# One transformer block on one core: big tiles at multiples of 512 bytes, one throw-away area for the score maxima

## The chip, the core and the metric

The kernel runs on one core of a Trainium2 chip. The core has four compute engines that run side by side, each with its own queue of instructions: TensorE (PE in the profile, with its weight loads as PEld), VectorE (DVE), ScalarE (ACT) and GpSimd (POOL). SyncE (SP) issues the DMA transfers here. Engines wait for each other by semaphores. SBUF, the working memory, has 128 partitions; a tile in it is an area of so many bytes in every partition, and "where a tile begins" is its offset in bytes within the partition. PSUM holds eight banks, in which PE accumulates its products (bank 0 to bank 7).

The metric is device time in microseconds (us) of one execution. Before the change it is 705.58 us, the median of 3 runs (704.65 to 707.68).

## The reference: what is computed

One pre-norm transformer block for 2048 tokens of width 448, in float32:

```
h   = x + attention(layernorm(x)) @ wo      # 16 heads of 28, causal window of 256 tokens
out = h + (gelu(n @ w_gate) * (n @ w_up)) @ w_down,  n = layernorm(h)     # inner width 1792
scores = (q @ k.T) / sqrt(28), outside the window -1e9, then softmax, then @ v
```

## The kernel before

**Arithmetic.** PE reads numbers that ACT has rounded ("high half", `to_hi` at L390) and, as a second operand, what is left over of the float32 number (the "low half", `to_lo` at L393, mostly on DVE). A product is then a sum of three: high by high, high by low and low by high.

**Stages.** The tokens lie in 16 tiles of 128. (1) Layer norm and the projection to q, k and v (L672, L618), with weights and tokens split in halves. (2) Attention, in 16 blocks B, each of 4 heads and 512 tokens. (3) The output projection (L894) and the sum into `hres`, the residual, which stays in SBUF as 16 x 448 floats per partition. (4) The second layer norm. (5) The feed-forward part in pairs of weight slices: products with the gate and up weights (L1128 and L1140 for the first pairs, L1329 for the others), GELU and the product on ACT, DVE and POOL, and the product with the down weights (L1403), whose results DVE adds into `hres` (L1420). The stages overlap: projections still run beside the first blocks of attention, the first feed-forward products beside the last ones. In the trace the scores of stage (2) run from about 40 to about 300 us, and the feed-forward part has PE for itself from about 312 us on.

**A block of attention.** For each of its 4 token tiles i and 4 heads j, PE computes 128 rows of scores against up to three key tiles (L723) into a PSUM bank. DVE adds the mask and takes the maximum of each row with one `tensor_tensor_reduce` (L727). Two things come out of that instruction: the maxima, into a column of `mx`, and the masked scores themselves, which nobody reads. These are written to `junk`. There are 16 of these steps per block, 256 in all, of 384 columns or fewer; in the built program each stands as two rows, the custom instruction and the reading of its accumulator. From `mx` DVE makes the high and low half of the maxima (L744, L747), PE turns them (L754), ACT puts them as further rows into `rq` (L390), and a second product (L798) then gives scores less their maximum, with keys down the partitions. ACT takes the exponent (L802), POOL sets what is outside the window to zero (L817), PE multiplies by v (L836).

**Where the buffers lie.** Three pools of tiles share SBUF. The main pool holds `hres`, `xT` (normed tokens, turned), `proj` (projection weights, later feed-forward weights and activations), `raw`, `v`, `xn` and small ones, and starts at the left. The pool "late" follows it: `rk1`, `rq1` (keys and queries of odd blocks), `mt` (the mask in columns 0 to 383, and the throw-away areas behind it), `pp` (probabilities), `oblk`, `oT`, `wos`, `ohl`; for the feed-forward part its place is taken by `xo` (tokens, turned) and `gh` (activations). The pool "even" grows from the right-hand end: `rk0` and `rq0` (even blocks), and later in their place `w2` and `e0` to `e3`. Feed-forward weights lie by turns in `w2` and in two areas of `proj`; in the profile's rows `w2` is called `w`, and the high halves of activations lie in `e` or `gh` or in parts of `xT`. PSUM banks 0 and 1 take the scores, and bank 7 as well once the projections are done.

**What sets the order.** The kernel computes the order itself. Each piece of work is put on a list with an engine, an assumed cost, a key (how early it is wanted) and the names it reads and writes; a list scheduler (class `Lists`) then writes the instructions out, engine by engine, and the framework keeps that order and adds the semaphores. Those it works out from the memory that the instructions touch. The scheduler's own names are apart from this: the score maxima are listed with a name `("junk", s % 2)` that they only read, before and after the change.

The lines that the change touches beside those in the functions below:

```
 276  last_hi = pool.tile([128, 128], F32R, name="lasthi")      # high half of a part of the turned tokens
 305  rp.tile([128, 88], F32, name="pad0")                      # ahead of rk0, rq0
 319  p.tile([128, 88], F32, name="pad1")                       # ahead of w2, e0 .. e3
 336  junk = [mt[:, 384 + 192 * i:576 + 192 * i].bitcast(BF) for i in range(2)]
```

Of the kernel before, what the change touches and what calls it, by code (L numbers as in the profile page):

```python
# [8 lines left out]
F32 = mybir.dt.float32  # L9
F32R = mybir.dt.float32r  # L10
BF = mybir.dt.bfloat16
# [79 lines left out]
def mm(n):  # L91
    return max(n / 2400 + 0.0155, 0.115)
# [14 lines left out]
class Lists:  # L107
# [6 lines left out]
    def op(self, eng, cost, lat, key, fn, r=(), w=(), bank=None, port=False, size=0, tag=None, after=(), part=None, mode=0):  # L114
        o = Op()
        o.eng, o.cost, o.lat, o.key, o.fn, o.port, o.size, o.tag, o.mode = eng, cost, lat, key, fn, port, size, tag, mode
        o.deps, o.users, o.ready, o.start = set(after), [], 0.0, None
        o.banks = () if bank is None else tuple(bank) if type(bank) is list else (bank,)
        for b in o.banks:
            b.left += 1  # L120
        held = o.banks if part is None else [(b, *part) for b in o.banks]
        if eng == "pe":
            w = (*w, *held)
        else:
            r = (*r, *held)
        for toks, wr in ((r, False), (w, True)):
            for tok in toks:
                spans = type(tok) is tuple and (tok[0] in SPANS or type(tok[0]) is Bank)
                name, lo, hi = tok if spans else (tok, 0, 1)
                old = self.seen.setdefault(name, [])  # L130
                keep = []
                for a in old:
                    if a[0] < hi and lo < a[1] and a[2] is not o:
                        if wr or a[3]:
                            o.deps.add(a[2])
                        if wr and lo <= a[0] and a[1] <= hi:
                            continue
                    keep.append(a)
                keep.append((lo, hi, o, wr))
                self.seen[name] = keep  # L140
        for d in o.deps:
            d.users.append(o)
        self.ops.append(o)
        if tag is not None:
            self.open[tag] = self.open.get(tag, 0) + 1
            self.all.setdefault(tag, []).append(o)
        return o
# [104 lines left out]
def block_kernel(ctx: ExitStack, tc, x, wqk_in, wv_in, wo_in, gu_in, rest_in, cw_in, down_in, out):  # L252
    nc = tc.nc
# [5 lines left out]
    pool = ctx.enter_context(tc.tile_pool(name="main", bufs=1))  # L259
# [4 lines left out]
        return ap.bitcast(F32)  # L264


    hres = pool.tile([128, NT, D], F32, name="hres")
    xT = pool.tile([128, 7, S], F32R, name="xT")
    proj_m = pool.tile([128, 7936], F32R, name="proj")
# [3 lines left out]
    xn = [xn_m[:, D * i:D * i + D] for i in range(2)]  # L273
    ident = pool.tile([128, 128], F32, name="ident")
    one_r = pool.tile([128, 128], F32R, name="one")
    last_hi = pool.tile([128, 128], F32R, name="lasthi")


    kept_m = pool.tile([128, 96], F32, name="kept")
# [19 lines left out]
    bank = [psum.tile([128, 512], F32, name=f"bank{i}") for i in range(8)]  # L299
# [2 lines left out]
    fst, snd = ExitStack(), ExitStack()  # L302
    lp = fst.enter_context(tc.tile_pool(name="late", bufs=1))
    rp = snd.enter_context(tc.tile_pool(name="even", bufs=1, side="right"))
    rp.tile([128, 88], F32, name="pad0")
    rks = [p.tile([128, 3072], F32R, name=f"rk{u}") for u, p in enumerate((rp, lp))]
    rqs = [p.tile([128, 2048], F32R, name=f"rq{u}") for u, p in enumerate((rp, lp))]
    mt = lp.tile([128, 768], F32, name="mt")
    pp_m = lp.tile([128, 4 * PPB * 128], F32, name="pp")
    oblk = lp.tile([128, 512], F32, name="oblk")  # L310
# [5 lines left out]
    def open_even():  # L316
        snd.close()
        p = ctx.enter_context(tc.tile_pool(name="ev", bufs=1, side="right"))
        p.tile([128, 88], F32, name="pad1")
        ev.append(p.tile([128, 3072], F32R, name="w2"))  # L320
        ev.extend(p.tile([128, 512], F32R if i > 1 else F32, name=f"e{i}") for i in range(4))

    def open_late():
        fst.close()
        p = ctx.enter_context(tc.tile_pool(name="fp", bufs=1))
        late.append(p.tile([128, 26 * 512], F32R, name="xo"))
        late.append(p.tile([128, 2, 2, 512], F32R, name="gh"))
# [5 lines left out]

    v = v_m[:, 0:8 * VT].rearrange("p (t h d) -> p t h d", t=8, h=H)
    mask = mt[:, 0:384]
    junk = [mt[:, 384 + 192 * i:576 + 192 * i].bitcast(BF) for i in range(2)]
    kept = [m.rearrange("p (b r) -> p b r", r=12) for m in (v_m[:, 8 * VT:8 * VT + 96], kept_m)]


# [350 lines left out]
    def block(B):  # L690
        return B % 4, B // 4
# [23 lines left out]
    def scores(B, i, j):  # L715
        g, c = block(B)
        u, m0 = B % 2, i if c else max(i, 2)
        b = Bank("score")
        o = (m0 - i) * 128
        s = 16 * B + 4 * i + j  # L720

        def one():
            nc.tensor.matmul(bank[b.k][:, o:384], rq[u][0:3 * DH, j, i * 128:i * 128 + 128],  # L723
                             rk[u][0:3 * DH, j, m0 * 128:(i + 3) * 128], start=True, stop=True)

        def most():
            nc.vector.tensor_tensor_reduce(junk[s % 2][:, o:384], bank[b.k][:, o:384], mask[:, o:384],  # L727
                                           1.0, -BIG, OP.add, OP.max, mx[:, i, j:j + 1])
        op("pe", mm(384 - o), 0.19 + (384 - o) / 2400, s, one,
           [("rq", u, i), *(("rk", u, m) for m in range(m0, i + 3))],  # L730
           (), b, tag="score")
        op("dve", 0.08 + (384 - o) * 0.00104, 0.165 + (384 - o) * 0.00106, s, most, ["mask", ("junk", s % 2)],
           [("mx", i, j)], b, tag="most")
# [883 lines left out]
    for c in range(CS):  # L1617
# [17 lines left out]
        for g in range(NG):  # L1635
# [30 lines left out]
            if B == 14:  # L1666
                op("py", 0, 0, 0, open_even, (), ["evenring"], after=[o for tag in ("score", "prob", "most", "tr", "rx") for o in L.all[tag]])
# [112 lines left out]
```

## Time and profile before

| what | value |
|---|---|
| median of 3 runs | 705.58 us (704.65 to 707.68) |
| the profiled execution | 707.69 us, of which the span from first to last instruction is 706.0 us |
| PE busy | 693.6 us, 98% of the span |
| DVE busy | 501.8 us, 71% |
| ACT / POOL busy | 414.7 us, 59% / 325.5 us, 46% |
| mean granted TensorE clock | 0.998 of full speed |
| stages: busy time of PE / DVE | 0 to 40 us: 37.2 / 31.7; 40 to 312 us: 272.0 / 211.6; 312 to 384 us: 69.4 / 44.2; 384 to 706 us: 315.0 / 214.2 |

How to read the rows that follow. A row of an instruction gives its start and its duration in us, its engine, the line of the kernel, the operation, and what it writes from what it reads. A row of a group gives a line, an engine, an operation and the tiles, the number of instructions (x), then busy time in us and the mean duration of one in ns, then the idle time of the engine just before them. A row of a stretch of time gives the stretch, the busy time of each engine with the number of instructions, the granted clock, the share of the DMA engines in use and what they moved. A row of waits says which engine waited at which tile and line, for whom, and how long: in all, how often, and the longest. "The chain" is the work that ended last, followed back from the last instruction to whatever released each step.

### The profile page before, as it was taken

To read this page: it belongs to the slowest core of one execution; us is meant where nothing else is said; L and a number is where in the kernel's file an instruction comes from. 1 tells how busy PE (TensorE), PEld (TensorE's weight loads), DVE (VectorE), ACT (ScalarE), POOL (GpSimd) and SP (SyncE) were. 2 spreads that over 40 slices of the span, in tenths; PEclk is the share of its full clock that TensorE was granted. 3 is DMA by queue.
4 is the path that set the end of the run, shared out by engine and by line. 5 is a ranking of instruction groups with operands and counts; after the bars stand their busy time and mean duration, and the time that the engine had idled before them with its cause. 6 is when DMAs were issued, how large, how long until landed. Compare 5 with 4: busy or idle time off the path is not lost.

```text
span 706.0 us, 15432 instructions
## 1 busy us (share of the span) xinstructions
PE 693.6 (98%) x5544; PEld 583.7 (83%) x5544; DVE 501.8 (71%) x1194; ACT 414.7 (59%) x911; POOL 325.5 (46%) x441
## 2 busy tenths in 40 slices
PE   8999999999999999999989999999999999999997
PEld 7887888877888787778778887888898888888886
DVE  7966668987796689838637677875745755865764
ACT  7746676877677666875544656635535445546431
POOL 5613544554546346441554678624403546657000
PEclk9999999999999999999999999999999999999999
DMA  8896967987678776306775866504304653442102
GB/s 310 269 292 187 294 176 216 217 233 189 193 228 222 211 206 173 109 1 163 197 194 174 243 187 188 148 15 129 89 1 128 188 165 121 139 145 86 42 15 104
DMA packets 104691, 116.25 MB, mean 165 GB/s; under 512 B 44632, under 2 KB 82392, under 8 KB 104040
## 3 DMA queue, kind: packets, MB, share of 16 engines
q1 hardware_dynamic: 104472, 115.17, 56.7%
q8 instruction: 43, 0.70, 0.4%
q14 instruction: 32, 0.26, 0.1%
q10 hardware_dynamic: 144, 0.11, 0.0%
HBM read 84.97 MB, written 44.47 MB: 183 GB/s over the span
## 4 chain that ended last, share of the span: by engine, by line
PE 92%; DVE 3%; DMA 2%; ACT 1%; issue 1%; SPq 0%; POOL 0%; DVEq 0%; ACTq 0%
PE bank L1329 26%; PE bank L1403 17%; PE bank L672 9%; PE bank L798 7%; PE bank L723 7%; PE bank L1128 6%; PE bank L836 6%; PE bank L894 5%; PE bank L618 5%; PE bank L1140 2%; DMA pp<-in_wv_dram 1%; DVE hres L1420 1%; DMA xn<-v 1%; PE bank L448 0%; DMA hres<-in_x_dram 0%
## 5 line engine op out<-in xcount | busy, mean ns | idle before, releaser
L727 DVE CUSTOM_DVE_ANT_0 mt<-bank,mt 128x384 bf16<-128x384 f32 (+2 forms) x256 | 127.0, 526 | 26.2 <-PE bank L723 24.1
L802 ACT ACTIVATE pp<-bank 128x384 f32<-128x384 f32 (+1 forms) x212 | 105.0, 536 | 26.6 <-PE bank L798 23.0
L817 POOL TENSOR_SCALAR_AFFINE_SELECT pp<-pp 128x512 f32<-128x512 f32 x120 | 75.9, 647 | 87.4 <-ACT pp L802 81.9
L1329 PE MATMUL bank<-xT,proj 64*128 64x512 f32 x735 | 94.5, 389 | 0.0
L672 PE MATMUL bank<-xT 128*128 128x512 f32 x308 | 93.0, 399 | 0.0
L1329 PEld LDWEIGHTS bank<-xT,proj 64*128 64x128 f32 x735 | 72.9, 184 | 11.9 <-ACT e L1249 0.4
L723 PE MATMUL bank<-rk,rq 84*128 84x384 f32 (+2 forms) x256 | 81.1, 340 | 0.0
L798 PE MATMUL bank<-rq,rk 104*128 104x384 f32 (+2 forms) x352 | 80.7, 305 | 0.0
L1403 PE MATMUL bank<-proj,gh 64*128 64x448 f32 x624 | 72.2, 363 | 0.1
L798 PEld LDWEIGHTS bank<-rq,rk 104*128 104x128 f32 x352 | 58.8, 189 | 12.2 <-ACT pp L802 3.6
L1420 DVE TENSOR_TENSOR hres<-bank,hres 128x448 f32<-128x448 f32 (+1 forms) x113 | 62.8, 611 | 5.8 <-PE bank L1403 5.7
L1403 PEld LDWEIGHTS bank<-proj,gh 64*128 64x128 f32 x624 | 60.0, 184 | 6.9 <-ACT e L1249 1.2
L1249 ACT ACTIVATE e<-bank 1x1 f32<-1x1 f32 x139 | 21.8, 157 | 69.6 <-PE bank L1403 45.7
L672 PEld LDWEIGHTS bank<-xT 128*128 128x128 f32 x308 | 55.7, 189 | 7.5 <-DVE proj L393 0.5
L723 PEld LDWEIGHTS bank<-rk,rq 84*128 84x128 f32 x256 | 47.0, 189 | 11.7 <-DVE xn L484 1.9
L1199 POOL TENSOR_TENSOR xn<-proj 128x384 f32<-128x384 f32 (+2 forms) x36 | 34.5, 961 | 46.5 <-DVE e L393 19.0
L390 ACT ACTIVATE rq<-bank 8x512 fp32r<-8x512 f32 x64 | 37.6, 588 | 23.2 <-PE bank L754 22.2
L618 PE MATMUL bank<-proj,xT 128*128 128x448 f32 (+1 forms) x220 | 50.0, 333 | 0.0
L1329 PE MATMUL bank<-xo,proj 64*128 64x512 f32 x366 | 48.1, 389 | 0.2 <-ACT e L1249 0.2
L393 DVE TENSOR_TENSOR proj<-proj 128x448 fp32r<-128x448 f32 (+2 forms) x32 | 24.0, 761 | 31.1 <-ACT proj L390 28.8
L836 PE MATMUL bank<-pp,v 128*29 128x384 f32 (+2 forms) x704 | 44.6, 387 | 0.0
L1403 PE MATMUL bank<-proj,xT 64*128 64x448 f32 x312 | 38.4, 368 | 4.4 <-ACT e L1249 2.5
(176 smaller groups left out, 1414.9 us busy)
## 6 DMA issues: line engine op xcount, KB each, us to landing
rk<-k SPq DMA_DIRECT2D x44, 336.0 KB
rq<-q SPq DMA_DIRECT2D x32, 336.0 KB
gu<-in_gu_dram SPq DMA_DIRECT2D x18, 480.0 KB
proj<-gu SPq DMA_DIRECT2D x24, 288.0 KB
q<-proj SPq DMA_DIRECT2D x12, 448.0 KB
proj<-down SPq DMA_DIRECT2D x22, 224.0 KB
proj<-gu SPq DMA_DIRECT2D x24, 192.0 KB
k<-proj SPq DMA_DIRECT2D x9, 448.0 KB
```

The lines of the kernel that those rows point to most:

```text
L618: op("pe", mm(224 * n), 0.29 if n == 1 else 0.38, key + a / 16, lambda a=a, h=h, wb=wb, xb=xb: nc.tensor.matmul(bank[b.k][:, 0:224 * n], x ...
L672: op("pe", mm(512) + 0.002, 0.403, key, lambda a=a, h=h, wb=wb, xb=xb: nc.tensor.matmul(bank[b.k], wqk[m][:, h, wb, :], xT[:, xb, cc * 128 ...
L723: nc.tensor.matmul(bank[b.k][:, o:384], rq[u][0:3 * DH, j, i * 128:i * 128 + 128], rk[u][0:3 * DH, j, m0 * 128:(i + 3) * 128], start=True, ...
L727: nc.vector.tensor_tensor_reduce(junk[s % 2][:, o:384], bank[b.k][:, o:384], mask[:, o:384], 1.0, -BIG, OP.add, OP.max, mx[:, i, j:j + 1])
L798: nc.tensor.matmul(bank[b.k][:, n * i:n * i + n], rk[u][0:104, j + i, m * 128:m * 128 + 128], rq[u][0:104, j + i, lo * 128:(hi + 1) * 128] ...
L802: nc.scalar.activation(pp[:, j:j + G, o * 128:o * 128 + n], bank[b.k][:, 0:G * n].rearrange("p (g t) -> p g t", g=G), AF.Exp, scale=SCALE)
L817: nc.gpsimd.affine_select(a, a, pattern=[[0, 4], [-cm, 128]], compare_op=op_, fill=0.0, base=0, channel_multiplier=cm)
L836: nc.tensor.matmul(bank[b.k][32 * j:32 * j + DH + 1, lo * 128:(hi + 1) * 128], v[:, at_v(4 * c - 2 + m), 4 * g + j, :], pp[:, j, at[m] * 1 ...
L1128: nc.tensor.matmul(bank[banks[side ^ ph].k], cwbuf[n % 4][0]()[HALF[side], o:o + 128], carea(c, xl, j, side), start=not ph and not j and n ...
L1329: nc.tensor.matmul(bank[b.k], w, xarea(u.cp, xl, xs, side)[:, xk], start=p in (1, 2, 5) and not k and not t, stop=t == 2, tile_position=(6 ...
L1403: nc.tensor.matmul(bank[banks[q].k][:, 0:D], h[oh][0]()[HALF[x], q * 128:q * 128 + 128], d[wh][0]()[HALF[x]], start=not ph and not y and n ...
L1420: op("dve", 0.07 + w * 0.463 / D, 0.163 + w * 0.463 / D, key, lambda: nc.vector.tensor_tensor(hres[:, t, c0:c0 + w], bank[b.k][:, c0:c0 + ...
```

## The change

```diff
--- before.py
+++ after.py
@@ -264,6 +264,7 @@
+    pool.tile([128, 96], F32, name="pad2")
     hres = pool.tile([128, NT, D], F32, name="hres")
     xT = pool.tile([128, 7, S], F32R, name="xT")
     proj_m = pool.tile([128, 7936], F32R, name="proj")
@@ -273,7 +274,6 @@
     ident = pool.tile([128, 128], F32, name="ident")
     one_r = pool.tile([128, 128], F32R, name="one")
-    last_hi = pool.tile([128, 128], F32R, name="lasthi")
@@ -302,9 +302,9 @@
     rp = snd.enter_context(tc.tile_pool(name="even", bufs=1, side="right"))
-    rp.tile([128, 88], F32, name="pad0")
     rks = [p.tile([128, 3072], F32R, name=f"rk{u}") for u, p in enumerate((rp, lp))]
     rqs = [p.tile([128, 2048], F32R, name=f"rq{u}") for u, p in enumerate((rp, lp))]
+    rp.tile([128, 120], F32, name="pad0")
@@ -316,9 +316,9 @@
-        p.tile([128, 88], F32, name="pad1")
         ev.append(p.tile([128, 3072], F32R, name="w2"))
         ev.extend(p.tile([128, 512], F32R if i > 1 else F32, name=f"e{i}") for i in range(4))
+        p.tile([128, 120], F32, name="pad1")
@@ -333,7 +333,8 @@
     mask = mt[:, 0:384]
-    junk = [mt[:, 384 + 192 * i:576 + 192 * i].bitcast(BF) for i in range(2)]
+    junk = mt[:, 384:576].bitcast(BF)
+    last_hi = mt[:, 576:704].bitcast(F32R)
@@ -724,7 +725,7 @@
-            nc.vector.tensor_tensor_reduce(junk[s % 2][:, o:384], bank[b.k][:, o:384], mask[:, o:384],
+            nc.vector.tensor_tensor_reduce(junk[:, o:384], bank[b.k][:, o:384], mask[:, o:384],
                                            1.0, -BIG, OP.add, OP.max, mx[:, i, j:j + 1])
```

**Where the tiles begin**, in bytes within the partition, as the remainder by 512, read from the built programs:

| tiles | before | after |
|---|---|---|
| `hres`, `xT`, `proj`, `raw`, `rk1`/`xo`, `rq1`, `mt`, `pp`, `oblk`, `oT`, `wos`, `ohl`/`gh` | 128 | 0 |
| `rk0`/`w2`, `rq0`/`e0` to `e3` | 480 | 0 |
| `v` | 384 | 256 |
| `xn`, `ident`, `one` | 256 | 128 |
| the halves of the maxima, `mhl` | 384 | 256 |

The new 384 bytes ahead of `hres` move the left-hand side. On the right-hand side a pool's tiles are packed against the end of SBUF in the order of their making, the last one outermost, so that a pad makes a difference to `rk0`, `rq0`, `w2` and `e` only if it is made after them. The 512 bytes of `last_hi` come out of the main pool; the tile now uses the part of `mt` that was the second throw-away area.

**One throw-away area.** Before, maximum s wrote its masked scores to area s % 2; now all of them write to the same 384 bf16 columns. Two maxima that follow each other now write the same memory, so the framework orders them by a semaphore, although both are on DVE and stand in the same order as before. On DVE's queue, early in attention (two low halves of tokens, then maxima from bank 0 and bank 1; `mt` is the tile with mask and throw-away area), there stands before:

```order
L393 TENSOR_TENSOR xT<-bank_178,xT 128x3x128 [waits Activation_49]
L393 TENSOR_TENSOR xT<-bank_178,xT 64x128
L727 ISA mt,mx<-bank_172,mt 128x384 [waits PE_49]
L727 ISA mx 128x1
L727 ISA mt,mx<-bank_173,mt 128x384 [waits PE_49]
```

and after (lines are one higher there):

```order
L394 TENSOR_TENSOR xT<-bank_178,xT 128x3x128 [waits Activation_49]
L394 TENSOR_TENSOR xT<-bank_178,xT 64x128
L728 ISA mt,mx<-bank_172,mt 128x384 [waits DVE_49,PE_49]
L728 ISA mx 128x1
L728 ISA mt,mx<-bank_173,mt 128x384 [waits DVE_49,PE_49]
```

No instruction has moved; each maximum waits for DVE itself beside PE. An instruction of this program carries one semaphore to wait for, and a second one becomes a semaphore instruction ahead of it: DVE has 1,648 instructions in the built program instead of 1,454. The order of PE, POOL, ACT and SP is the same as before, and so are the waits of PE, POOL and SP.

## The prediction

> **What bounds the kernel now.** I read the head of the page first, then the chain that ended last, then the busy time by stretches, then the instructions one by one.
>
> ```profile
> span 706.0 us, 15432 instructions
> PE 693.6 (98%) x5544; PEld 583.7 (83%) x5544; DVE 501.8 (71%) x1194; ACT 414.7 (59%) x911; POOL 325.5 (46%) x441
> PE 92%; DVE 3%; DMA 2%; ACT 1%; issue 1%; SPq 0%; POOL 0%; DVEq 0%; ACTq 0%
> ```
>
> PE is busy in 98% of the span and carries 92% of the chain. So a nanosecond of PE's pace counts, and so does any moment in which PE waits for another engine; work elsewhere counts only through such a wait. The change touches both: it moves the tiles that PE reads, and it ties each score maximum on VectorE (DVE) to the one before it. The attention phase, where the maxima are, has these rows (columns: PE, PEld, DVE, ACT, POOL busy, clock, DMA share, GB/s):
>
> ```profile
> 40.00:300.00 260.00, 259.97 (x1805) 209.41 (x1804) 207.02 (x701) 182.74 (x360) 123.77 (x204) 1.00 0.75 209
> 120.00:130.00 10.00, 10.00 (x69) 7.96 (x68) 9.16 (x31) 9.22 (x21) 3.73 (x5) 1.00 0.74 199
> 140.00:150.00 10.00, 10.00 (x72) 6.97 (x74) 9.70 (x31) 8.11 (x19) 6.48 (x10) 1.00 0.68 214
> 200.00:210.00 10.00, 10.00 (x71) 8.96 (x73) 9.95 (x37) 8.13 (x16) 5.74 (x13) 1.00 0.81 260
> 260.00:270.00 10.00, 10.00 (x90) 7.65 (x89) 9.83 (x32) 7.17 (x14) 3.25 (x6) 1.00 0.91 239
> 270.00:280.00 10.00, 10.00 (x72) 8.22 (x71) 8.78 (x33) 7.43 (x16) 8.31 (x16) 1.00 0.39 113
> 280.00:290.00 10.00, 9.99 (x69) 6.99 (x68) 8.80 (x31) 7.41 (x15) 3.38 (x7) 1.00 0.79 223
> ```
>
> PE shows no idle time at all here. DVE is busy 207.0 of 260 us on the mean, but nearly full in places (9.95 of 10 us at 200). DVE is the second engine of this phase, and it is the one that the change loads.
>
> **The waits, step by step.** First the price of one. Instructions of DVE that depend on the one before them, and ones that do not, stand side by side here (start, duration):
>
> ```profile
> 32.76 0.59 DVE L422 BATCH_NORM_STATS2 bnst<-hres 128x6 f32<-128x448 f32 x1
> 33.45 0.18 DVE L424 BATCH_NORM_AGGREGATE bnmv<-bnst 128x2 f32<-128x6 f32 x1
> 33.55 0.60 DVE L422 BATCH_NORM_STATS2 bnst<-hres 128x6 f32<-128x448 f32 x1
> 34.18 0.18 DVE L424 BATCH_NORM_AGGREGATE bnmv<-bnst 128x2 f32<-128x6 f32 x1
> ```
>
> The first aggregate reads what the statistics wrote and waits for another engine too, so its wait on DVE is an instruction of its own: it starts at 33.45, 0.10 us after the statistics end (32.76 + 0.59 = 33.35). The next statistics depend on nothing near: they start at 33.55, 0.08 us before the aggregate ends (33.63). The second aggregate has the wait on DVE alone: 34.18, 0.03 us after 34.15. The maxima after the change wait on PE and on DVE, hence the first form: from 0.08 us before the end to 0.10 us after it, 0.18 us.
>
> The rows of the maxima: each is a custom instruction and a reading of its accumulator.
>
> ```profile
> 41.54 0.28 DVE L727 CUSTOM_DVE_ANT_0 mt<-bank,mt 128x128 bf16<-128x128 f32 x1
> ...
> 272.00 0.08 DVE L727 DVE_READ_ACCUMULATOR2_ANT mx<- 128x1 f32 x1
> 272.00 0.55 DVE L727 CUSTOM_DVE_ANT_0 mt<-bank,mt 128x384 bf16<-128x384 f32 x1
> ...
> 296.51 0.55 DVE L727 CUSTOM_DVE_ANT_0 mt<-bank,mt 128x384 bf16<-128x384 f32 x1
> ```
>
> At 272.00 the second maximum starts together with the reading of the first, which ends at 272.08. With the new wait it could start at 272.08 + 0.10 = 272.18, so it loses 0.18 us. Of 256 maxima, 173 follow another directly. In the trace 103 of these start with the reading, as here (the first at 41.54, the last at 296.51), and lose 0.18 us each, 19.0 us in all; 29 start a little later and lose a part, 2.2 us; the other 41 already stand behind a longer wait for PE and lose nothing. Maxima with another DVE instruction in between lose nothing, since the earlier one has long ended. Sum: 21.2 us more time on DVE's queue, which therefore delays all that stands behind a maximum on it: low halves of weights and tokens, evictions of the output projection, and the next maxima.
>
> How much of 21.2 us reaches the end? The upper bound is all of it: PE has no idle time to give back. The lower bound is 0: DVE has 53 us of idle time in the phase (260 - 207). What decides is how far DVE may run late. Scores alternate between two banks (three near the end), and a tile comes about once a microsecond (256 in 256 us), so PE stalls when DVE is one or two microseconds behind. Over 10 us the waits add 0.92, 0.82, 1.11, 0.92, 1.46 and 1.27 us in the six stretches quoted; busy time and addition exceed 10 us there by 0.08, 0.52, 1.06, 0.75, 0.24 and 0.07, together 2.7 us that cannot be hidden. Over 5 us the same count gives 5.9 us in fifteen stretches, the first and last of which are:
>
> ```profile
> 105.00:110.00 5.00, 5.00 (x30) 4.55 (x29) 5.00 (x18) 4.19 (x11) 3.71 (x5) 1.00 0.86 263
> 285.00:290.00 5.00, 4.99 (x25) 3.78 (x25) 4.64 (x15) 4.89 (x11) 1.29 (x2) 1.00 0.55 119
> ```
>
> Since the slack is nearer to 2 us than to 10, I take the 5-us count: **+6 us**, with 2.7 and 21.2 kept as ends.
>
> **The addresses, step by step.** No big tile of before begins at a multiple of 512, so the trace cannot show the new place. It shows two old ones: 480 past a multiple (rk, rq, w2 and e on the right-hand side) and 128 past it (proj, xT, xo, gh). The same products from the two places:
>
> ```profile
> 511.92 2.22 PE L1329 MATMUL bank<-xo,proj 64*128 64x512 f32 x18
> 513.96 1.40 PE L1403 MATMUL bank<-proj,e 64*128 64x448 f32 x12
> 515.19 2.22 PE L1329 MATMUL bank<-xo,proj 64*128 64x512 f32 x18
> 517.23 1.39 PE L1403 MATMUL bank<-proj,gh 64*128 64x448 f32 x12
> 518.44 2.24 PE L1329 MATMUL bank<-xo,proj 64*128 64x512 f32 x18
> ...
> 522.39 2.27 PE L1329 MATMUL bank<-xT,w 64*128 64x512 f32 x18
> 524.49 1.39 PE L1403 MATMUL bank<-proj,xT 64*128 64x448 f32 x12
> ```
>
> From start to start, 18 matmuls with weights in proj take 513.96 - 511.92 = 2.04 us, with weights in w2 524.49 - 522.39 = 2.10 us: 0.06 us more. Twelve with activations in e take 1.23 us, in gh 1.21 us: 0.02 us more. If the new place is as good as 128, the rows to which this applies are:
>
> ```profile
> L1329 PE MATMUL bank<-xT,w 64*128 64x512 f32 x294 | 39.4, 392 | 0.0
> L1329 PE MATMUL bank<-xo,w 64*128 64x512 f32 x222 | 30.3, 393 | 0.1
> L1128 PE MATMUL bank<-xT,w 64*128 64x512 f32 x84 | 10.3, 393 | 0.0
> L1403 PE MATMUL bank<-proj,e 64*128 64x448 f32 x312 | 36.7, 363 | 0.1
> L1403 PE MATMUL bank<-w,e 64*128 64x448 f32 x24 | 2.6, 363 | 0.0
> ```
>
> 600 / 18 x 0.06 = 2.0 us and 336 / 12 x 0.02 = 0.5 us: a gain of at most 2.5 us. A part is eaten where PE then waits for what was not sped up:
>
> ```profile
> PEld bank L1403 <- ACT e L1249: 4.1, 4, 2.8
> PEld bank L1403 <- DVE xT L393: 2.1, 1, 2.1
> ```
>
> I take **-1 us**, between 0 and -2.5. For the tiles that go from 128 to 0 I take nothing; the bounds are a like gain (rival below) and a like loss. That ACT, DVE and DMA work faster from the new places I take as nothing too: they are off the chain but for 7% of it. The Trainium skill, page "SBUF — State Buffer", section "Specifications (TRN2)", gives cache lines of 16 bytes; all places here, old and new, are multiples of 32 bytes, so by that rule nothing would be gained, and the sum would be 1 us higher. The trace does not agree: 2.10 against 2.04 us. last_hi only moves into mt: its four copies stay, at no cost.
>
> **The sum.** +6 - 1 = +5 us. The profiled execution took 707.69 us, 706.0 of span and 1.7 around it, which is 2.1 above the median of 705.58. Against its own time the change gives 712.7, against the median **710.5 us**.
>
> **Rivals.**
> ```profile
> DVE mt L727 <- PE bank L723: 24.1, 49, 2.5
> PEld bank L723 <- DVE mx L727: 1.2, 4, 0.6
> PE bank L1329 26%; PE bank L1403 17%; PE bank L672 9%; PE bank L798 7%; PE bank L723 7%; PE bank L1128 6%; PE bank L836 6%; PE bank L894 5%; PE bank L618 5%; PE bank L1140 2%; DMA pp<-in_wv_dram 1%; DVE hres L1420 1%; DMA xn<-v 1%; PE bank L448 0%; DMA hres<-in_x_dram 0%
> ```
>
> (a) No change that can be measured (0.5%, 3.5 us, is about what a measurement tells). DVE's idle time takes the waits but for the 10-us count: +2.7, less 1 to 2.5, gives 706 to 707. For it: 53 us of idle time, and the first row above: DVE waits 24.1 us for scores (in all, times, longest). Against it: PE's row without idle time. A variant is that a wait is free because the pipeline has to empty anyway; then the sum is -1 to -2.5, or 703 to 705. The Trainium skill says so in "VectorE: DVE Perf Modes", section "The DRAIN you can't avoid": eight copies took the same time with a semaphore after each and with one after the last. The trace does not agree: unheld instructions start 0.08 us before the end of the one in front, held ones 0.03 or 0.10 us after it. I give 0.27 to (a), of which 0.04 to the variant.
> (b) Faster. If every matmul of the feed-forward gains from 128 to 0 what those in w2 and e gained from 480 to 128: L1329 and L1128 hold 26% and 6% of the chain in the last row above, 32% of 706 = 226 us, or 111 groups of 2.04, 6.6 us at 0.06 each; L1403 holds 17%, 120 us, or 99 groups of 1.21, 2.0 us at 0.02 each. With the 2.5 us that makes 11.1, and with the waits at +6 the time is 700.5. It decides once the pace gains over 9.5 us. For it: place does matter to PE in one row. Against it: 480 is no multiple of 64 where 128 and 0 both are, so what those tiles gained may be all there is. 0.07.
> (c) Slower still. Around 260 to 297 us maxima come in runs and DVE is 88 to 98% full, so lateness adds up instead of being worked off: half of 21.2 us, +10.6 - 1, gives 715, all of it 726. 0.08 for over 717.
> (d) The forecast, 709.1 to 717: 0.58.
>
> A further unknown is the clock. After PE's longest gap it runs at half speed for 3.2 us, worth 1.6 us; moved, this may go or come twice:
>
> ```profile
> 359.00:362.00 3.00, 1.18 (x10) 1.13 (x12) 0.00 (x0) 2.67 (x7) 2.16 (x2) 0.96 1.00 324
> 362.00:365.20 3.20, 3.20 (x18) 2.55 (x18) 1.82 (x3) 0.64 (x1) 1.58 (x2) 0.50 0.46 153
> ```
>
> **The numbers.** Faster by over 0.5% is (b): 0.07. Within it is (a): 0.27. Slower is (c) and (d): 0.66. The range 703 to 717 holds (a) and (d) and leaves out (b) and (c), 0.15 together; the forecast's own range is 709 to 717.
>
> **What would show it.** In the trace after: maxima that start 0.18 us after their neighbour's reading begins instead of with it (0.47 us apart now, 0.65 then); some 190 more semaphore instructions of that line; DVE waiting less for scores than 24.1 us; score matmuls whose weight load waits for the maxima more than the 1.2 us of now; 18 matmuls from w2 in 2.04 instead of 2.10 us; the loss complete by 312 us. I am wrong if the attention phase ends as early as now, if 18 matmuls from proj leave 2.04 us, or if the time comes back after 312 us.

## The result and the profile after

The changed kernel takes 717.62 us (median of 6 runs, 716.14 to 718.40) where the kernel before, run beside it, takes 706.45. The ratio is 1.0147, with a 95% interval of 1.013 to 1.0165: slower by 10.4 us (9.2 to 11.7). The two medians lie 11.2 us apart, within that interval; the spans of the two profiled executions, 716.4 and 706.0 us, lie 10.4 us apart. The direction was forecast, the size was not: 5 us were expected, and the time lies above the range.

The head of the page of the changed kernel, then three of its groups (busy time, mean ns of one, then the idle time ahead of them and what ended it; lines are one higher than before):

```profile
span 716.4 us, 15626 instructions
PE 701.4 (98%) x5544; PEld 575.9 (80%) x5544; DVE 516.8 (72%) x1194; ACT 415.5 (58%) x911; POOL 324.3 (45%) x441
PE 84%; DVE 7%; DMA 3%; issue 2%; ACT 2%; POOL 1%; SPq 0%; DVEq 0%; ACTq 0%
L728 DVE CUSTOM_DVE_ANT_0 mt<-bank,mt 128x384 bf16<-128x384 f32 (+2 forms) x256 | 135.1, 528 | 35.3 <-PE bank L724 11.3
L724 PE MATMUL bank<-rk,rq 84*128 84x384 f32 (+2 forms) x256 | 88.8, 366 | 1.8 <-DVE mx L728 1.1
L724 PEld LDWEIGHTS bank<-rk,rq 84*128 84x128 f32 x256 | 46.7, 188 | 30.5 <-DVE mx L728 21.6
```

DVE's share of the chain has gone from 3 to 7%. In the wait list of the changed kernel (who waited, where, for whom: us in all, times, longest) the weight loads of the scores now wait 71 times for the maxima, 21.6 us in all, where it was 4 times and 1.2 us; and DVE waits for scores 11.3 us instead of 24.1:

```profile
PEld bank L724 <- DVE mx L728: 21.6, 71, 1.0
...
DVE mt L728 <- PE bank L724: 11.3, 18, 2.6
```

Where the time was lost is seen at a landmark. The last product with v (L836, then L837) ends the attention phase. Timeline of the kernel before, then of the changed one (start, duration, instructions):

```profile
314.19 1.50 PE L836 MATMUL bank<-pp,v 128*29 128x384 f32 x24
```

```profile
327.87 1.50 PE L837 MATMUL bank<-pp,v 128*29 128x384 f32 x24
```

It comes 13.7 us later. Since PE's instructions stand in the same order in both kernels, each can be matched with itself: the changed kernel is behind by 2.2 us where the old one is at 100 us, by 5.4 at 150, 7.1 at 200, 8.8 at 250 and 13.6 at 300. The loss grows all through attention, about a third of it in the last 50 us. Behind the landmark it shrinks to the 10.4 us of the spans; two reasons are given below.

The stretch from 40 to 312 us, before and then after (busy time of PE, PEld, DVE, ACT, POOL with instructions, clock, DMA share, GB/s):

```profile
40.00:312.00 272.00, 271.97 (x1902) 218.63 (x1901) 211.62 (x708) 192.62 (x379) 129.86 (x214) 1.00 0.72 200
```

```profile
40.00:312.00 272.00, 268.74 (x1797) 203.48 (x1796) 217.49 (x699) 183.15 (x359) 123.82 (x204) 1.00 0.68 198
```

PE gets through 1,797 products there instead of 1,902 and still shows 268.7 of 272 us as busy. That is the trap in this view: only 3 of some 14 lost us appear as idle time. The rest hides in the records of the products, as the next rows show.

**One turn of a score bank.** Timeline of the kernel before, the rows of scores and maxima alone:

```profile
104.71 0.52 DVE L727 CUSTOM_DVE_ANT_0 mt<-bank,mt 128x384 bf16<-128x384 f32 x1
105.16 0.09 DVE L727 DVE_READ_ACCUMULATOR2_ANT mx<- 128x1 f32 x1
105.16 0.56 DVE L727 CUSTOM_DVE_ANT_0 mt<-bank,mt 128x384 bf16<-128x384 f32 x1
105.39 0.19 PEld L723 LDWEIGHTS bank<-rk,rq 84*128 84x128 f32 x1
105.56 0.34 PE L723 MATMUL bank<-rk,rq 84*128 84x384 f32 x1
105.64 0.09 DVE L727 DVE_READ_ACCUMULATOR2_ANT mx<- 128x1 f32 x1
105.92 0.19 PEld L723 LDWEIGHTS bank<-rk,rq 84*128 84x128 f32 x1
106.16 0.34 PE L723 MATMUL bank<-rk,rq 84*128 84x384 f32 x1
```

The same place in the changed kernel:

```profile
107.12 0.52 DVE L728 CUSTOM_DVE_ANT_0 mt<-bank,mt 128x384 bf16<-128x384 f32 x1
107.57 0.08 DVE L728 DVE_READ_ACCUMULATOR2_ANT mx<- 128x1 f32 x1
107.71 0.19 PEld L724 LDWEIGHTS bank<-rk,rq 84*128 84x128 f32 x1
107.78 0.37 PE L724 MATMUL bank<-rk,rq 84*128 84x384 f32 x1
107.80 0.56 DVE L728 CUSTOM_DVE_ANT_0 mt<-bank,mt 128x384 bf16<-128x384 f32 x1
108.28 0.08 DVE L728 DVE_READ_ACCUMULATOR2_ANT mx<- 128x1 f32 x1
108.42 0.19 PEld L724 LDWEIGHTS bank<-rk,rq 84*128 84x128 f32 x1 [0.23 <-DVE mx L728]
108.42 0.45 PE L724 MATMUL bank<-rk,rq 84*128 84x384 f32 x1
```

Three things are to be read here. First, the second maximum starts at 107.80, 0.15 us after the reading that ended at 107.65; before, it started with that reading (105.16). Second, what waits for the bank on PE is the weight load of the next score, not the product: at 108.42 it starts 0.06 us after the reading ends (108.36). Before, the same load started at 105.92, 0.19 us after its reading (105.73), and its own 0.19 us lay beside a product that was still running. Third, with the load held back, the product is recorded as starting with it (108.42) and lasting 0.45 instead of 0.34 us: waiting that the busy time counts as work. Over all 256 scores the mean record grew from 340 to 366 ns, some 6.7 us in all.

Counted over all turns of a bank (253, with the banks as the kernel's own order gives them out), from the end of a reading to the start of the next weight load of a score for that bank: the smallest value is 0.05 us in both kernels. Before, a quarter of the values are at most 0.14 us and half at most 0.27; after, half are at most 0.06. Less than 0.10 us are 45 before and 148 after. Taking the smallest value as what the handover itself needs, in a quarter of all turns there were at most 0.09 us to spare, and in half at most 0.22: no more than what one of the new waits costs (0.226 us, see below). The expectations further down say 0.09 us for half of the loads; by this count it is a quarter.

**Behind the landmark.** The longest gap of PE was followed by 3.2 us at half the clock before. In the changed kernel the same stretch, 13 us later:

```profile
371.90:375.00 3.10, 1.03 (x10) 0.96 (x12) 0.00 (x0) 2.93 (x7) 2.01 (x2) 1.00 0.83 237
375.00:378.20 3.20, 3.20 (x32) 2.65 (x30) 1.99 (x3) 0.95 (x3) 1.75 (x2) 1.00 0.74 240
```

The clock stays at 1.00, and 1.6 us come back there. By PE's own instructions another 1.3 us come back behind the landmark, and the pace of the feed-forward products accounts for at least a part of them. (The figure is good to about 1 us: the kernel of the first experiment below has the old addresses, and matched in the same way its lag drifts between 13.1 and 14.4 us behind the landmark.) Two groups of the changed kernel (least, median and largest ns of one):

```profile
L1330 PE MATMUL bank<-xT,w x294: 383/386/501, 533.9 to 667.4; 64*128 64x512 f32 x147
L1330 PE MATMUL bank<-xT,proj x735: 383/386/502, 479.4 to 694.3; 64*128 64x512 f32 x184
```

Products with weights in w2 take 386 ns like those in proj, where they took 392 before; those in proj are unchanged.

### The profile page after: what moved, and what is told of

It is laid out like the page before. It is cut to its first block, busy times and chain, and to the rows that moved or that the text cites. A ratio compares the mean times of both kernels' runs of the same rounds, so it can differ in the third digit from the quotient of the medians.

```text
span 716.4 us, 15626 instructions
## 1 busy us (share of the span) xinstructions
PE 701.4 (98%) x5544; PEld 575.9 (80%) x5544; DVE 516.8 (72%) x1194; ACT 415.5 (58%) x911; POOL 324.3 (45%) x441
## 4 chain that ended last, share of the span: by engine, by line
PE 84%; DVE 7%; DMA 3%; issue 2%; ACT 2%; POOL 1%; SPq 0%; DVEq 0%; ACTq 0%
PE bank L1330 26%; PE bank L1404 17%; PE bank L673 8%; PE bank L724 7%; PE bank L799 6%; PE bank L1129 5%; PE bank L837 5%; PE bank L895 5%; PE bank L619 4%; DVE mt L728 3%; PE bank L1141 1%; DVE xT L394 1%; DVE hres L1421 1%; DMA hres<-in_x_dram 1%; DMA xl<-xn 1%
## 5 line engine op out<-in xcount | busy, mean ns | idle before, releaser
L728 DVE CUSTOM_DVE_ANT_0 mt<-bank,mt 128x384 bf16<-128x384 f32 (+2 forms) x256 | 135.1, 528 | 35.3 <-PE bank L724 11.3
L724 PE MATMUL bank<-rk,rq 84*128 84x384 f32 (+2 forms) x256 | 88.8, 366 | 1.8 <-DVE mx L728 1.1
L1330 PEld LDWEIGHTS bank<-xT,proj 64*128 64x128 f32 x735 | 73.5, 184 | 11.2 <-DVE v L1340 0.4
L724 PEld LDWEIGHTS bank<-rk,rq 84*128 84x128 f32 x256 | 46.7, 188 | 30.5 <-DVE mx L728 21.6
L391 ACT ACTIVATE rq<-bank 8x512 fp32r<-8x512 f32 x64 | 37.6, 588 | 25.1 <-PE bank L755 24.1
L394 DVE TENSOR_TENSOR proj<-proj 128x448 fp32r<-128x448 f32 (+2 forms) x32 | 25.6, 810 | 29.3 <-ACT proj L391 27.7
L837 PE MATMUL bank<-pp,v 128*29 128x384 f32 (+2 forms) x704 | 44.6, 387 | 0.0
L1330 PEld LDWEIGHTS bank<-xo,proj 64*128 64x128 f32 x366 | 36.6, 184 | 6.9 <-ACT e L1250 0.6
```

Of the source, the lines that this page charges most:

```text
L391: nc.scalar.activation(dst, src, AF.Copy)
L728: nc.vector.tensor_tensor_reduce(junk[:, o:384], bank[b.k][:, o:384], mask[:, o:384], 1.0, -BIG, OP.add, OP.max, mx[:, i, j:j + 1])
L837: nc.tensor.matmul(bank[b.k][32 * j:32 * j + DH + 1, lo * 128:(hi + 1) * 128], v[:, at_v(4 * c - 2 + m), 4 * g + j, :], pp[:, j, at[m] * 1 ...
L1330: nc.tensor.matmul(bank[b.k], w, xarea(u.cp, xl, xs, side)[:, xk], start=p in (1, 2, 5) and not k and not t, stop=t == 2, tile_position=(6 ...
```

## The experiments

Theory A came from the rows above: the weight load of a score waits for its bank, there is hardly anything to spare, and so DVE's new waits reach PE. Theory B keeps the prediction's sum (+6 us for the waits) and puts the other 7.7 us down to the new addresses.

### Each half of the change alone

One area at the old addresses:

```diff
-            nc.vector.tensor_tensor_reduce(junk[s % 2][:, o:384], bank[b.k][:, o:384], mask[:, o:384],
+            nc.vector.tensor_tensor_reduce(junk[0][:, o:384], bank[b.k][:, o:384], mask[:, o:384],
```

> The kernel before with one throw-away area and nothing else: every tile stays where it was. Theory A (the score banks come back too late: the weight load of a score product waits for its bank, and in the trace of before half of these loads start within 0.09 us of the earliest time they could, so nearly each 0.18 us of wait on VectorE reaches TensorE): the waits alone give the whole loss of the attention phase of the changed kernel, +13.7 us at its end, and a time 12 to 14 us over before. Theory B (the prediction's count over 5 us was right, and the other 7.7 us come from the new addresses of the attention tiles): +6 us here.

The new addresses with two areas (edits against the changed kernel):

```diff
-    junk = mt[:, 384:576].bitcast(BF)
-    last_hi = mt[:, 576:704].bitcast(F32R)
+    junk = [mt[:, 384 + 192 * i:576 + 192 * i].bitcast(BF) for i in range(2)]
+    last_hi = ident.bitcast(F32R)
...
-            nc.vector.tensor_tensor_reduce(junk[:, o:384], ...
+            nc.vector.tensor_tensor_reduce(junk[s % 2][:, o:384], ...
```

> The changed kernel with all tiles at their new places, but two throw-away areas again (the high half last_hi goes to the tile ident, whose last reader ends at 49.6 us, 67 us earlier). Theory A: the attention phase ends as in before, the products from w2 and e run at the pace of those from proj, 1 to 1.5 us faster than before in all. Theory B: 6 to 7 us slower than before, all of it before 312 us.

One area alone: 721.05 us against 707.93, ratio 1.0198 (1.0178 to 1.0218). The landmark and two waits of that kernel:

```profile
328.03 1.50 PE L836 MATMUL bank<-pp,v 128*29 128x384 f32 x24
```

```profile
PEld bank L723 <- DVE mx L727: 21.5, 71, 1.0
DVE mt L727 <- PE bank L723: 11.3, 18, 2.5
```

328.03 is 13.8 us after the 314.19 of before: the whole loss of the attention phase is there without a tile being moved. The waits are those of the changed kernel to a tenth of a microsecond. Theory B falls.

The new addresses alone: 705.78 us against 707.93, ratio 0.9975 (0.9959 to 0.9991). Its landmark:

```profile
313.83 1.50 PE L837 MATMUL bank<-pp,v 128*29 128x384 f32 x24
```

0.4 us earlier than before. The addresses cost nothing by the end of attention; as a whole this kernel is a little faster than before, by 1.8 us (0.6 to 2.9).

### Which addresses count

The right-hand pools' pads were moved, so that rk0, rq0, w2 and e begin at 128 past a multiple of 512, and then at 192 past one; two areas, everything else as before. The edit for 128, made alike for the pad of w2 and e; for 192 it is a pad of 16 columns ahead and one of 72 behind:

```diff
-    rp.tile([128, 88], F32, name="pad0")
     rks = [p.tile([128, 3072], F32R, name=f"rk{u}") for u, p in enumerate((rp, lp))]
     rqs = [p.tile([128, 2048], F32R, name=f"rq{u}") for u, p in enumerate((rp, lp))]
+    rp.tile([128, 88], F32, name="pad0b")
```

> The kernel before with the pads of the right-hand pools behind the tiles instead of ahead of them: rk0, rq0, w2 and e begin 128 past a multiple of 512 like the rest, two areas. If it is 480 that is slow and not 128: products from w2 at 386 ns instead of 392, and 1 to 1.5 us faster than before, as much as with all tiles at multiples of 512. If only multiples of 512 are fast: no change from before.

> As the last, with the right-hand tiles at 192 past a multiple of 512, a multiple of 64 but not of 128. If a multiple of 64 is enough, products from w2 take 386 ns; if it has to be a multiple of 128 or 512, 392 as in before.

The same group at 128 past and then at 192 past:

```profile
L1329 PE MATMUL bank<-xT,w x294: 383/386/493, 521.4 to 655.0; 64*128 64x512 f32 x147
```

```profile
L1331 PE MATMUL bank<-xT,w x294: 385/394/465, 522.3 to 656.3; 64*128 64x512 f32 x147
```

So 128 and 0 are fast (386 ns), 480 (392) and 192 (394) are not: of the four places tried, the two at multiples of 128 bytes are the good ones; 192, a multiple of 64, and 480, a multiple of 32, are not. The kernel at 192 ran once (707.61 us), which gives no comparison of times. The prediction's argument that 480 is slow because it is no multiple of 64 falls. The Trainium skill, page "SBUF — State Buffer", section "Specifications (TRN2)", speaks of cache lines of 16 bytes, each crossing of which has a price; all four places begin such a line, so the difference seen here is another one.

As a time the placement at 128 could not be told from no change: ratio 0.9994 (0.9979 to 1.0009). The faster pace is certain in the records. What it is worth lies between the 0.4 us of that ratio, the 1.8 of the kernel at multiples of 512, and the 3.6 that lie between 1.0147 and 1.0198. The clock moves a single run as much: of 23 runs of before in this comparison, 13 with a mean granted clock of 0.999 or 1.000 have a median of 706.84 us, and 10 with 0.998 or less one of 708.72.

### How the loss grows with the number of waits

The two areas change after every second maximum, in two ways, so that a part of the neighbours is held:

```diff
-            nc.vector.tensor_tensor_reduce(junk[s % 2][:, o:384], ...
+            nc.vector.tensor_tensor_reduce(junk[s // 2 % 2][:, o:384], ...           # pairs_even
+            nc.vector.tensor_tensor_reduce(junk[(s + 1) // 2 % 2][:, o:384], ...     # pairs_odd
```

> The kernel before, with the two areas changing after every second maximum: maxima 0 and 1 share one, 2 and 3 the other. By the trace of before 94 maxima (101 neighbours) are then held, for 14.4 us of VectorE time in all, instead of 132 for 20.6 us. Theory A (a run of maxima passes on what it is late, less the 0.09 us by which the banks come back early, once a run): 7 to 8 us at the end of attention. Rival F (a fixed share of 66%, as in the full change): 9.5 us. Rival B (only what overflows 5 us of VectorE time): 3 to 4 us.

> As the last with the pairs shifted by one (maxima 1 and 2 share an area, 3 and 4 the other): 38 maxima are held, for 6.3 us of VectorE time. Theory A: about 3 us at the end of attention. Rival F: 4.2 us, so that both halves add up to the 13.7 us of the whole. Rival B: 1 us or less.

Landmark and DVE's waiting for scores, even pairs and then odd ones:

```profile
321.82 1.50 PE L836 MATMUL bank<-pp,v 128*29 128x384 f32 x24
```

```profile
DVE mt L727 <- PE bank L723: 15.1, 27, 2.5
```

```profile
316.90 1.50 PE L836 MATMUL bank<-pp,v 128*29 128x384 f32 x24
```

```profile
DVE mt L727 <- PE bank L723: 21.4, 43, 2.5
```

| kernel | maxima delayed | time added on DVE | less waiting for scores on DVE | landmark later by | ratio to before |
|---|---|---|---|---|---|
| odd pairs | 40 | 8.1 us | 2.7 us | 2.7 us | 1.0028 (1.0012 to 1.0043) |
| even pairs | 95 | 18.7 us | 9.0 us | 7.6 us | 1.0099 (1.0072 to 1.0127) |
| one area | 135 | 26.8 us | 12.8 us | 13.8 us | 1.0198 (1.0178 to 1.0218) |

The added time is worked out from the trace of before, with each held maximum starting 0.144 us after the end of the reading in front, as measured below. The share that reaches PE rises from a third to a half, and the halves make 10.3 us together where the whole makes 13.8: neither a fixed share (F) nor what overflows 5 us (B). Theory A's figures (7 to 8 us, and about 3) were met, but in part by luck, since its price of 0.18 us was too low and its spare time of 0.09 us too. With the measured price, a count that lets each run of maxima pass on its added time less 0.09 us gives 5.5, 13.2 and 19.9 us for the three kernels, and less 0.22 us 1.8, 5.5 and 9.9; the measured values lie between. So no single figure of spare time fits; it differs too much from turn to turn. The columns in the middle say where the added time goes: into waiting for scores that DVE is spared, and into lateness of PE. For one area the two make 26.6 of the 26.8 us; for odd pairs they make only 5.4 of 8.1, and where the other 2.7 went was not followed up.

### Is it the fullness of DVE, or the turn of the banks?

Two pairs of kernels take about the same time off DVE, once away from the maxima and once inside them, each with two areas and with one:

```diff
-            hres[:, t, :], bank[k.k][:, 0:D], hres[:, t, :], op=OP.add), ...          # short_others, with bn_stats alike
+            hres[:, t, 0:8], bank[k.k][:, 0:8], hres[:, t, 0:8], op=OP.add), ...
...
-            nc.vector.tensor_tensor_reduce(junk[s % 2][:, o:384], bank[b.k][:, o:384], mask[:, o:384],   # short_max
+            nc.vector.tensor_tensor_reduce(junk[s % 2][:, o:304], bank[b.k][:, o:304], mask[:, o:304],   # _one: junk[0]
```

> The kernel before with less of other work on VectorE: the sum of the output projection into hres (L897) and the layer norm statistics (L422) take 8 columns of 448, which leaves out the rest of both and takes some 21 us off VectorE between 40 and 312 us, none of it from the maxima. Two areas. It is the base for the next kernel: 0 to 4 us faster than before.

> The last kernel with one area (the same parts of L897 and L422 left out). The loss is against the last kernel, at the end of attention. Theory A: the score banks still come back 0.18 us late in each run, 11 to 14 us. Theory C (VectorE has too little idle time in this phase): 20.6 us of waits find 21 us of new room, and the loss falls under 5 us.

> The kernel before with maxima over 80 columns less (304 instead of 384; the maximum of the last 80 columns is left out), so that each takes 0.08 us less: 21 us less on VectorE, as much as in the pair before, all of it from the maxima. Two areas. Base for the next kernel: 0 to 6 us faster than before, since half of the weight loads of scores start within 0.09 us of the release of their bank.

> The last kernel with one area (the same 80 columns left out). The loss is against the last kernel, at the end of attention. Theory A: a bank that comes back 0.08 us sooner covers half of a wait, so 4 to 8 us, well under the pair with other work shortened. Theory C: the same VectorE time is free as there, so the same loss as there.

Busy time from 40 to 312 us with other work shortened, then with the maxima shortened, both with two areas: DVE has 196.8 and 195.0 us, 14.8 and 16.6 less than before (some 21 were expected of each).

```profile
40.00:312.00 272.00, 271.97 (x1901) 218.34 (x1900) 196.84 (x707) 192.84 (x380) 130.10 (x214) 1.00 0.73 200
```

```profile
40.00:312.00 272.00, 271.97 (x1904) 218.94 (x1903) 195.01 (x708) 192.91 (x379) 129.79 (x214) 1.00 0.73 200
```

Landmarks, in the order short_others two and one, short_max two and one:

```profile
313.94 1.50 PE L836 MATMUL bank<-pp,v 128*29 128x384 f32 x24
```

```profile
323.54 1.50 PE L836 MATMUL bank<-pp,v 128*29 128x384 f32 x24
```

```profile
314.11 1.50 PE L836 MATMUL bank<-pp,v 128*29 128x384 f32 x24
```

```profile
316.37 1.50 PE L836 MATMUL bank<-pp,v 128*29 128x384 f32 x24
```

With other work shortened, one area still costs 9.6 us; with the maxima shortened, 2.3 us. Theory C, by which only DVE's total counts, would have them alike: it falls. Theory A has the order right and both sizes wrong (11 to 14 and 4 to 8 were expected). Room elsewhere on DVE takes away more than it allowed, 4.2 of 13.8 us, and 0.08 us off each maximum takes away 11.5, much more than half. The waits for scores tell how much was taken up, in the same order:

```profile
DVE mt L727 <- PE bank L723: 29.4, 63, 2.6
```

```profile
DVE mt L727 <- PE bank L723: 14.3, 25, 2.5
```

```profile
DVE mt L727 <- PE bank L723: 35.5, 68, 2.6
```

```profile
DVE mt L727 <- PE bank L723: 20.3, 41, 2.6
```

15.1 and 15.2 us, against 12.8 without shortening: equal amounts. In the last pair the waits also added less, since more maxima stood behind a later wait for PE anyway: worked out as in the table above, from the traces of the two kernels with two areas, 25.7 us are added with other work shortened and 21.1 with the maxima shortened. So of the 7.3 us between the two losses at most 4.6 can come from there, and theory C still falls. As times the four gave ratios to before of 0.998 (0.9961 to 0.9999), 1.0121 (1.0101 to 1.0141), 0.9988 (0.9971 to 1.0005) and 1.0023 (1.0009 to 1.0036).

The third of these is a finding of its own: maxima that are 0.08 us shorter bring the landmark forward by 0.1 us. The kernel before stood on an edge. Banks coming back sooner gain it nothing, and banks coming back later cost it about half of the added time (13.8 of 26.8 us).

## Why the prediction was wrong in size

**The kind of wait: right.** The semaphore instructions of the line went from 42 to 236, 194 more where some 190 were named. Before and after, in the instruction list of that line on DVE's sequencer:

```profile
L727 DVEq EVENT_SEMAPHORE  x42: 21/21/21, 54.7 to 295.9; - x42
```

```profile
L728 DVEq EVENT_SEMAPHORE  x236: 21/21/21, 41.6 to 310.5; - x118
```

**Its price: too small.** The step took 0.10 us after the end in front, from one statistics pair. Of the 170 maxima that directly follow another in the changed kernel (the prediction counted 173), the median starts 0.144 us after the reading (least 0.144; 162 are between 0.12 and 0.16). From 0.08 us before to 0.144 after is 0.226 us instead of 0.18, and in place of the 21.2 us of the sum 26.8 are added. The page "VectorE: DVE Perf Modes" of the Trainium skill, section "The DRAIN you can't avoid", says that a semaphore between copies costs nothing; the measurement decides against it for a maximum that waits for the one directly in front.

**What of it reaches the end: the step that failed.** "Since the slack is nearer to 2 us than to 10, I take the 5-us count" gave 6 of 21.2 us; measured are 13.7 of 26.8. With the right price the count over 5 us gives about 8, over 2.5 us 13, over 1.25 us 17.5. So of the 7.7 us missed, some 2 are the price and the rest, over 5.5, the slack. The step did not even follow its own estimate: with a slack of one or two microseconds the count, at its own price, would have been over 2.5 us (9.6) or 1.25 us (13.3). That estimate was itself too large. It had been taken from how often a score comes, about one in a microsecond on the mean. But PE asks for the bank with the weight load, ahead of the product, and between release and load there were at most 0.22 us to spare in half the turns, not 2 us; besides, the pairs of the third experiment fit a lateness that DVE passes on from one maximum to the next of a run. The number stood in the trace of before, in rows of PEld that were not read, such as the load at 105.39 behind the reading that ended at 105.25.

**"PE shows no idle time at all here": read wrongly.** That row was taken to mean that PE has nothing to give back, which holds. But it cannot show waiting either, since records of products stretch over it.

**The addresses: right, as far as can be told.** Products from w2 went from 392 to 386 ns, proj stayed at 386, and nothing was gained from 128 to 0. Against the -1 us of the sum stand, by matching PE's instructions, 1.3 us in the changed kernel without the clock's share (good to about 1 us), and in the comparison of times 1.8 (0.6 to 2.9) with two areas.

**The clock** was named as unknown, worth 1.6 us; here it gave them back, so that the whole is +13.7 - 1.6 - 1.3 = +10.8 by PE's instructions, and +10.4 by the spans.

**The rivals.** (a), no change, and (b), faster, did not occur. The time of 717.62 lies in (c), slower still, which had 0.08. Its own figure at half of the waits, 715, lay inside the forecast's range, so that only its upper part could differ from the forecast. Its mechanism is half right: lateness adds up in runs of maxima. Its place is not: 260 to 297 us hold 3.9 of the 13.7 us. That the loss would be complete by 312 us was right but for the shift of 14 us, and 3 of the 13.7 us came back later by the clock and the pace.

## What to carry to other kernels

Before two uses of a buffer are merged, look whether neighbours on one engine come to write the same memory: the wait that orders them cost up to 0.226 us each here, for results that nobody reads. To judge what such a delay does, measure the spare time at the handover itself, from release to the first instruction of the other engine that needs it (here a weight load, not its product); busy shares and mean rates of the stage did not show it here. And a matmul engine that is "98% busy" may still be waiting: compare the mean record of one instruction, 340 against 366 ns.

## What was not expected of the hardware

- A wait on DVE for an instruction three or more places back costs nothing. Two maxima of the kernel before, the second of which waits for the reading that ends at 259.51, three places in front:

```profile
259.42 0.09 DVE L727 DVE_READ_ACCUMULATOR2_ANT mx<- 128x1 f32 x1
259.58 0.56 DVE L727 CUSTOM_DVE_ANT_0 mt<-bank,mt 128x384 bf16<-128x384 f32 x1
260.07 0.08 DVE L727 DVE_READ_ACCUMULATOR2_ANT mx<- 128x1 f32 x1
260.07 0.55 DVE L727 CUSTOM_DVE_ANT_0 mt<-bank,mt 128x384 bf16<-128x384 f32 x1
```

It starts with the reading of its neighbour (260.07), like maxima without a wait. Of the 42 that wait on DVE in that kernel, 31 start 0.075 to 0.086 us before the end of the instruction in front. In the changed kernel 49 maxima carry the new wait with one other DVE instruction between them and the reading in front, and 44 of them start 0.075 to 0.085 us before the end of that instruction. So neither the wait nor its semaphore instruction costs anything as such; only the wait for the instruction directly in front has a price.
- PE's products of 64 x 128 weights with 512 columns take 386 ns with weights at 0 or 128 past a multiple of 512 bytes, 392 at 480 and 391 or 394 at 192 (medians of two groups), while the weight loads themselves take 184 or 185 ns in all four.
- The half-clock stretch after the longest gap of PE does not belong to a kernel: it was in the profiled run of before, where it lowers the mean granted clock to 0.998, but 6 of the 23 runs of before that are compared above have a mean of 1.000 and so cannot have had it.
